# Every load of a decode-attention kernel in two halves of its columns, on two DMA queues

## Chip, cores, metric

One core of one Trainium2 chip. The metric is the device time of one execution in microseconds; lower is better.

## The reference

One token goes through four attention layers, which use two sets of caches and weights (A, B, A, B). Each layer reads all of its keys and values once, for a single query:

```python
# x: 1 x 1 x 640; 32 heads of 192; 8192 cached positions; all bf16
def _A_ref(x, k_cache, v_cache, wq, wo):                       # _B_ref is the same
    q = (x @ wq).reshape(B, Sq, Hq, Dh).transpose(0, 2, 1, 3)
    p = softmax(einsum("bhqd,bhkd->bhqk", q, k) * Dh ** -0.5)
    o = einsum("bhqk,bhkd->bhqd", p, v)
    return o.transpose(0, 2, 1, 3).reshape(B, Sq, Hq * Dh) @ wo
x = x + _A_ref(layernorm(x), ...)      # then B, then A again, then B again
```

## The kernel before

The kernel handles heads in pairs. Keys or values of a pair are 6.3 MB: 128 partitions with one contiguous row of 49,152 B each. They are loaded into a pool of eight slots of 24,576 B per partition; a slot is loaded again as soon as its reader is done.

Instructions are collected per engine, in program order. An operation first adds the waits for the events it needs to its engine's stream. `SP` is SyncE, `AC` ScalarE, `DV` VectorE (DVE), `PE` TensorE.

```python
class Queue:
    def op(self, fn, *events, sem=None, inc=1, signal=True, bank=()):
        ...
        self.wait(*events)                       # in front of fn, in this engine's stream
        ...
        self.counts[id(sem)] = self.counts.get(id(sem), 0) + inc
        self.items.append((fn, sem, inc))
        return sem, self.counts[id(sem)]         # the event: "sem has reached this count"
```

All loads but that of x are issued by SyncE, each as one transfer:

```python
def transfer(n):                                 # n: what to load, e.g. ("k", layer, pair, half)
    free = [freed[b] for b in before[n]]         # the readers of what lay in these slots
    ...
    if n[0] in "kv":
        h = 2 * pair(l, n[2])
        r = w[n[0]][0, h:h + 2].rearrange("h (p j) d -> (h p) (j d)", j=J)
        ...
        if whole(*n[:3]):                        # both slots in one transfer, 49,152 B a row
            f = lambda s: s.dma_start(pool[:, i * TS:(i + 2) * TS], r)
        else:                                    # one slot, 24,576 B a row
            f = lambda s: s.dma_start(t, r[:, n[3] * TS:(n[3] + 1) * TS])
    ...                                          # wq and wo in the same way
    return SP.op(f, *free, sem=semS[i], inc=16)

def ahead():                                     # after every step of the program:
    while issued[0] < len(plan):                 # load what is next in the plan,
        m = plan[issued[0]]
        if any(b not in freed for b in before[m]):
            return                               # as far as its slots' readers are in the program
        issued[0] += 1
        landed[m] = transfer(m)

ev_x = AC.op(lambda s: s.dma_start(x_bf[:], A_x[0, 0].rearrange("(p c) -> p c", c=DC)), sem=semX, inc=16)
ahead()
```

For each pair DVE multiplies the keys by the query, PE sums the products (reading the key slots), DVE and PE find the maximum, ScalarE takes the exponentials, PE multiplies by the values (reading the value slots), and DVE, PE and ScalarE gather the result in a row. ScalarE also copies the next pair's query (`q_sb`).

Of the kernel before, what the change touches and what calls it, by code (L numbers as in the profile page):

```python
# [63 lines left out]
PAIRS_W = 5  # L64
# [4 lines left out]
def build(nc, A_x, A_k, A_v, A_wq, A_wo, B_x, B_k, B_v, B_wq, B_wo, out):  # L69
    _, H, SK, DH = A_k.shape  # L70
    D = A_x.shape[-1]
    P = 128
    J = 2 * SK // P
    JU = J // 2
    DC = D // P
# [6 lines left out]
    PD = 2 * DH  # L82
    NW = PAIRS_W * PD // P
    QC = (NPAIR - 1) * PD
    QR = QC // 3
    TS = JU * DH
    QW = H * DH
    Q_PARTS = [(0, 2), (2, 2), (4, 1)]
    OI = PD // P
    NB = [0, 5, 0, 5]  # L90
# [4 lines left out]
                    wo=[NPAIR - PAIRS_W, 1, 1 + PAIRS_W], wol=0)  # L95
    ORDER = [FORWARD, FORWARD, FORWARD, BACKWARD]

    with ExitStack() as ctx:
        def sb(name, shape, dt):
            return ctx.enter_context(nc.sbuf_tensor(name, shape, dt))  # L100
# [4 lines left out]
        def sem(name):  # L105
            return ctx.enter_context(nc.semaphore(name))

        ident = sb("ident", [P, P], BF16)
        pool = sb("pool", [P, NSLOT * TS], BF16)
        slot = [pool[:, i * TS:(i + 1) * TS] for i in range(NSLOT)]  # L110
        wq0 = [sb(f"wq0{i}", [P, DC, PD], BF16) for i in range(2)]
        rows = sb("rows", [P, QR], BF16)
# [56 lines left out]
        AC = Queue(sem("pACT"))  # L169
        PO = Queue(sem("pPOOL"))  # L170
        SP = Queue()
        semS = [sem(f"semS{i}") for i in range(NSLOT)]
        semOL, semOB, semVQ, semX, semOUT = [sem(n) for n in ("semOL", "semOB", "semVQ", "semX", "semOUT")]

        e = PO.op(lambda g: g.memset(ident[:], 0.0))
# [6 lines left out]
        e = PO.op(lambda g: g.memset(mask, 0.0))  # L182
        for t in range(G):
            e = PO.op(lambda g, t=t: g.affine_select(
                out=mask, in_=mask, compare_op=ALU.not_equal, fill=1.0,
                base=-32 * t, pattern=[[-1, 2], [-2, VK]], channel_multiplier=1), e)
# [10 lines left out]
        def pair(l, p):  # L197
            return ORDER[l]["pairs"][p]
# [11 lines left out]
        def whole(kind, l, p):  # L210

            if kind == "t":
                return False
            if kind == "k":
                return l < 2 and p not in (PAIRS_W, 2 * PAIRS_W) or l == 3 and p > 1
            if p == NPAIR - 1:
                return False
            return l != 2 or p not in (0, PAIRS_W, 2 * PAIRS_W)
# [7 lines left out]
        for l in range(NL):  # L226
# [8 lines left out]
            for p in range(NPAIR):  # L235
# [17 lines left out]
                if p < NPAIR - 2:  # L253
                    if first_load("v", l, p) == (l, p):
                        plan += [("v", l, p, u) for u in range(2)]
                        if l == 2 and p == 1:
                            i = plan.index(("k", l, 1, 0))
# [33 lines left out]
        place, before, holder = {}, {}, [None] * NSLOT  # L291
# [29 lines left out]
        for i, n in list(enumerate(plan)):  # L321
            if n[0] == "v" and n[3] == 0:
                m = n[:3] + (1,)
# [8 lines left out]
        def wq_rows(l, g):  # L332

            c0, k = Q_PARTS[g]
            if l < 2:
                i = place[("wq", l, 0)] * TS
                return pool[:, i + c0 * QW:i + (c0 + k) * QW].rearrange("p (c n) -> p c n", c=k)
            return slot[place[("wq", l, g)]][:, 0:k * QC].rearrange("p (c n) -> p c n", c=k)

        def quarters(n):  # L340
            return n[0] == "v" and n[2:] == (NPAIR - 1, 1) and NB[n[1]] > 0

        def transfer(n):
            l = n[1]
            o = ORDER[l]
            w = W[l % 2]
            free = [freed[b] for b in before[n]]
            if n[0] == "wol":
                r0 = o["wol"] * PD
                return SP.op(lambda s: s.dma_start(  # L350
                    rows[:], w["wo"][r0:r0 + PD].rearrange("(p i) n -> p (i n)", p=P)),
                    *free, sem=semOL, inc=16)
            if n[0] == "t":
                return max(free, key=lambda e: e[1]) if free else None
            if n[0] == "wob":
                r0 = o["wo"][2] * PD
                return SP.op(lambda s: s.dma_start(
                    slot[place[("wo", l, 2)]][:, (NW - NB[l]) * D:NW * D],
                    w["wo"][r0:r0 + PAIRS_W * PD].rearrange("(p i) n -> p (i n)", p=P)[:, (NW - NB[l]) * D:]),
                    sem=semOB, inc=16)  # L360
            if n[0] == "vq":
                n = ("v", l, NPAIR - 1, 1)
            i = place[n]
            t = slot[i]
# [3 lines that stand above are left out]
                if quarters(n):  # L368
                    x = TS // 2
                    if n in landed:  # L370
                        return SP.op(lambda s: s.dma_start(t[:, x:], r[:, TS + x:]), sem=semVQ, inc=16)
                    return SP.op(lambda s: s.dma_start(t[:, 0:x], r[:, TS:TS + x]), *free, sem=semS[i], inc=16)
                if whole(*n[:3]):
                    if n[3] == 1:
                        return landed[n[:3] + (0,)]
                    f = lambda s: s.dma_start(pool[:, i * TS:(i + 2) * TS], r)
                else:
                    f = lambda s: s.dma_start(t, r[:, n[3] * TS:(n[3] + 1) * TS])
            elif n[0] == "wq" and l < 2:
                f = lambda s: s.dma_start(pool[:, i * TS:i * TS + DC * QW], w["wq"].rearrange("(p c) n -> p (c n)", c=DC))  # L380
            elif n[0] == "wq":
                c0, k = Q_PARTS[n[2]]
                f = lambda s: s.dma_start(
                    wq_rows(l, n[2]),
                    w["wq"][:, o["q1"] * PD:o["q1"] * PD + QC].rearrange("(p c) n -> p c n", c=DC)[:, c0:c0 + k, :])
            else:
                r0 = o["wo"][n[2]] * PD
                k = NW - NB[l] if n[2] == 2 else NW
                f = lambda s: s.dma_start(
                    t[:, 0:k * D], w["wo"][r0:r0 + PAIRS_W * PD].rearrange("(p i) n -> p (i n)", p=P)[:, 0:k * D])  # L390
            return SP.op(f, *free, sem=semS[i], inc=16)

        def need(n):

            while n not in landed:
# [3 lines that stand above are left out]
            return landed[n]  # L399

        def ahead():

            while issued[0] < len(plan):
                m = plan[issued[0]]
                if any(b not in freed for b in before[m]):
                    return
                issued[0] += 1
                landed[m] = transfer(m)
# [357 lines left out]
        for l in range(NL):  # L766
            ev_z, ev_true = layer(l, ev_z, ev_true)
        e = SP.op(lambda s: s.dma_start(out[0, 0].rearrange("(h n) -> h n", h=2), ev_z[0:33:32, :]), *ev_true, sem=semOUT, inc=16)
        SP.wait(e)
# [10 lines left out]
def bass_interleave_layers__gqa_block_cached__mha_block_cached__decode_kernel(  # L780
    nc: bass.Bass,
    A_x: bass.AP,
    A_k_cache: bass.AP,
    A_v_cache: bass.AP,
    A_wq: bass.AP,
    A_wo: bass.AP,
    B_x: bass.AP,
    B_k_cache: bass.AP,
    B_v_cache: bass.AP,
    B_wq: bass.AP,  # L790
    B_wo: bass.AP,
    out: bass.AP,
):
    build(nc, A_x, A_k_cache, A_v_cache, A_wq, A_wo, B_x, B_k_cache, B_v_cache, B_wq, B_wo, out)
# [28 lines left out]
```

## Time and profile before

| | before |
|---|---|
| median of 4 runs | 1983.51 us (1983.18 to 1985.16) |
| profiled span | 1980.6 us |
| loaded from HBM | 848.36 MB, 428 GB/s over the span |
| DMA packets | 26,786, nearly all on one queue (q1) |
| busy: PE, DVE, ACT | 65%, 61%, 7% |

The page gives busy shares of each engine, GB/s in 40 slices, and the packets that each DMA queue moved: a packet here is one partition's row of a transfer, or the 4 bytes that report a completion. Its lines stand in the prediction below.

### The profile page before, as it was taken

How to read it: one execution, taken by the hardware profiler on the slowest of the kernel's cores; microseconds unless marked ns; L12 is line 12 of the kernel's file. 1: busy time of each engine (PE TensorE's matmuls, PEld its weight loads, DVE VectorE, ACT ScalarE, POOL GpSimd, SP SyncE). 2: the span in 40 equal slices, each digit the busy share in tenths (PEclk: the TensorE clock that was granted, in tenths of full speed). 3: DMA queues.
4: the chain of work that ended last, by engine and by line, in shares of the span. 5: the costliest groups of instructions: out<-in, count | busy, mean ns of one | idle time of the engine just before them, and what ended most of it. 6: DMA issues, size and time to landing. Idle time of an engine off the chain costs nothing.

```text
span 1980.6 us, 13926 instructions
## 1 busy us (share of the span) xinstructions
PE 1282.8 (65%) x8335; PEld 148.6 (8%) x3249; DVE 1201.2 (61%) x1377; ACT 139.6 (7%) x462; POOL 4.5 (0%) x23
## 2 busy tenths in 40 slices
PE   3567476566466666666785675666676766667658
PEld 0001001000100100100020010010002001001001
DVE  3566466467166656566745565665764765665756
ACT  0000000000000000000010000000000100000000
POOL 0000000000000000000000000000000000000000
PEclk9787777778687777777887777877886877777778
DMA  9999999999999999999999999999999999999998
GB/s 413 437 432 430 430 430 432 436 430 428 435 431 431 430 435 433 428 433 433 427 408 432 427 430 431 430 430 431 431 431 428 436 429 434 432 432 431 431 434 364
DMA packets 26786, 849.25 MB, mean 429 GB/s; under 512 B 3042, under 2 KB 3044, under 8 KB 3812
## 3 DMA queue, kind: packets, MB, share of 16 engines
q1 hardware_dynamic: 26580, 848.38, 99.6%
q8 instruction: 45, 0.74, 0.2%
q14 instruction: 17, 0.14, 0.0%
q10 hardware_dynamic: 144, 0.00, 0.0%
HBM read 848.36 MB, written 0.00 MB: 428 GB/s over the span
## 4 chain that ended last, share of the span: by engine, by line
DMA 67%; PE 17%; DVE 15%; ACT 1%; issue 0%; SPq 0%
DMA pool<-in_B_k_cache_dram 27%; DMA pool<-in_A_v_cache_dram 22%; DMA pool<-in_A_k_cache_dram 13%; DVE pool L595 13%; PE S L58 7%; DMA pool<-in_B_v_cache_dram 6%; PE OY L58 5%; PE OY L674 3%; DVE acc L693 1%; ACT p_sb L632 1%; DVE s_sb L617 1%; PE OY L535 1%; PE S L608 0%; DVE m_bf L619 0%; PE QM L622 0%
## 5 line engine op out<-in xcount | busy, mean ns | idle before, releaser
L595 DVE TENSOR_TENSOR pool<-pool,q_sb 128x3072 bf16<-128x3072 bf16 x512 | 860.8, 1751 | 231.9 <-DMA pool<-in_B_k_cache_dram 133.3
L58 PE MATMUL S<-pool,ident 128*128 128x512 bf16 x2944 | 788.6, 425 | 20.4 <-DVE pool L595 18.8
L704 PE MATMUL TB<-acc,small 128*1 128x192 f32 x240 | 82.7, 495 | 212.0 <-DVE acc L693 212.0
L58 PE MATMUL OY<-pool,p_sb 128*16 128x512 bf16 x1920 | 198.8, 490 | 0.0
L608 PE MATMUL S<-pool,ident 128*128 128x512 bf16 x128 | 62.4, 488 | 207.7 <-DVE pool L595 207.6
L692 DVE TENSOR_SCALAR acc<-OY,small 128x192 f32<-128x192 f32 x64 | 26.7, 418 | 277.9 <-PE OY L58 248.0
L674 PE MATMUL OY<-pool,p_sb 128*16 128x512 bf16 (+1 forms) x1216 | 145.9, 488 | 64.3 <-DMA pool<-in_A_v_cache_dram 59.7
L693 DVE SCALAR_TENSOR_TENSOR acc<-OY,small,acc 128x192 f32<-128x192 f32 x424 | 177.0, 418 | 14.9
L617 DVE TENSOR_REDUCE s_sb<-S 128x64 f32<-128x512 f32 x128 | 87.8, 686 | 68.0 <-PE S L58 68.0
L524 ACT ACTIVATE q_sb<-QM 128x192 bf16<-128x192 f32 x60 | 19.8, 330 | 952.4 <-PE QM L518 952.4
L715 ACT ACTIVATE rows<-TB,small 1x192 bf16<-1x192 f32 x120 | 43.1, 405 | 587.7 <-PE TB L704 587.7
L688 DVE RECIPROCAL small<-TB 1x2 f32<-1x2 f32 x64 | 11.2, 175 | 94.7 <-PE TB L647 75.3
L632 ACT ACTIVATE p_sb<-s_sb,small 64x128 bf16<-64x128 f32 x128 | 55.7, 435 | 160.9 <-DVE small L626 160.1
L608 PEld LDWEIGHTS S<-pool,ident 128*128 128x128 bf16 x128 | 12.9, 101 | 682.9 <-DVE pool L595 619.9
L647 PE MATMUL TB<-small,ones 128*1 128x2 f32 x120 | 11.4, 165 | 74.1 <-ACT p_sb L632 74.1
L674 PEld LDWEIGHTS OY<-pool,p_sb 128*16 128x16 bf16 (+1 forms) x1216 | 38.9, 105 | 207.4 <-issue 133.1
L622 PE MATMUL QM<-ident,m_bf 128*64 128x64 bf16 x128 | 14.1, 217 | 54.4 <-DVE m_bf L619 53.8
L704 PEld LDWEIGHTS TB<-acc,small 128*1 128x1 f32 x240 | 19.8, 102 | 311.2 <-DVE acc L693 284.0
L535 PE MATMUL OY<-oT,pool 128*128 128x1 bf16 x825 | 34.9, 178 | 2.5 <-ACT oT L580 2.5
L626 DVE TENSOR_REDUCE small<-QM 128x1 f32<-128x64 f32 x64 | 14.3, 224 | 35.2 <-PE QM L622 35.2
L535 PEld LDWEIGHTS OY<-oT,pool 128*128 128x128 bf16 x825 | 33.9, 131 | 4.5 <-ACT oT L580 3.2
L518 PEld LDWEIGHTS QM<-rows,one_b 1*64 1x64 bf16 x120 | 6.2, 100 | 347.1 <-issue 341.2
(75 smaller groups left out, 205.0 us busy)
## 6 DMA issues: line engine op xcount, KB each, us to landing
pool<-in_B_k_cache_dram SPq DMA_DIRECT2D x28, 6144.0 KB, 38.1
pool<-in_B_v_cache_dram SPq DMA_DIRECT2D x28, 6144.0 KB, 33.5
pool<-in_A_v_cache_dram SPq DMA_DIRECT2D x27, 6144.0 KB, 27.6
pool<-in_A_k_cache_dram SPq DMA_DIRECT2D x34, 3072.0 KB, 19.9
pool<-in_A_k_cache_dram SPq DMA_DIRECT2D x14, 6144.0 KB, 36.5
pool<-in_A_v_cache_dram SPq DMA_DIRECT2D x10, 3072.0 KB, 14.3
pool<-in_B_k_cache_dram SPq DMA_DIRECT2D x8, 3072.0 KB, 22.4
pool<-in_A_wo_dram SPq DMA_DIRECT2D x6, 2400.0 KB, 22.1
```

Of the source, the lines that this page charges most:

```text
L58: return t.add_instruction(mybir.InstMatmult(name=t.bass.get_next_instruction_name(), engine=mybir.EngineType.PE, ins=[t.lower_ap(rhs), t. ...
L524: lambda a: a.activation(q_sb[i][:], QM[:, 0:DH], ACT.Copy), e, last["q"][i], bank=QMu)
L535: e = PE.op(lambda t, i=i, c=c, f=y_first[0], fin=n[0] == "wol" and i == k - 1: t.matmul(YB[:, c:c + 1], lhsT=t3[:, i, c:D:DC], rhs=o[:, i ...
L595: e = DV.op(lambda v, d0=d0: v.tensor_tensor(k3[:, :, d0:d0 + QD], kin[:, :, d0:d0 + QD], q_sb[qi][:, d0:d0 + QD].unsqueeze(1).broadcast_t ...
L608: t.matmul(S[:, :], lhsT=ident[:], rhs=k3[:, :, d0:d0 + R], start=True, stop=fin) if d0 == 0 else
L617: lambda v, u=u: v.tensor_reduce(s[:, u * JU:(u + 1) * JU], SP_[u][:].rearrange("p (j r) -> p j r", r=R), AX.X, ALU.add), ev_S[p, u], last ...
L632: ev_p[p] = AC.op(lambda a, h=h, r=r: a.activation(p_sb[par][r, :, h], s[r, :], ACT.Exp, bias=negm[par][r, 0:1], accum_out=l_col[par][r, h ...
L674: t.matmul(o, lhsT=x, rhs=y, start=f, stop=fin) if c == 0 else
L692: v.tensor_scalar(acc[:], O[:, 0:DH], pick[:, 0:1], None, ALU.mult) if i == 0 else
L693: v.scalar_tensor_tensor(out=acc[:], in0=O[:, i * DH:(i + 1) * DH], scalar=pick[:, i:i + 1], in1=acc[:], op0=ALU.mult, op1=ALU.add)), e if ...
L704: e = PE.op(lambda t, h=h: t.matmul(TB[96:97, C_O + h * DH:C_O + (h + 1) * DH], lhsT=half[:, h:h + 1], rhs=acc[:], start=True, stop=True), ...
L715: last["TO"] = last["row_written"] = AC.op(lambda a, h=h: a.activation(orow[:, o0 + h * DH:o0 + (h + 1) * DH], TB[96:97, C_O + h * DH:C_O ...
```

## The change

Every load becomes two, each of half the columns over all 128 partitions; one half is issued by SyncE, the other by ScalarE, on the same semaphore. The intent is to have two queues feed the DMA engines and two engines issue. The two queues now add to the same semaphores, so they share one table of counts.

```diff
         SP = Queue()
+        SP.counts = AC.counts
...
             free = [freed[b] for b in before[n]]
+
+            def move(dst, src, sem):
+
+                if len(dst.shape) == 3 and dst.shape[1] == 2:
+                    parts = [(slice(None), i) for i in range(2)]
+                else:
+                    m = dst.shape[-1] // 2
+                    parts = [(slice(None),) * (len(dst.shape) - 1) + (c,) for c in (slice(0, m), slice(m, 2 * m))]
+                for q, x in zip((SP, AC), parts):
+                    e = q.op(lambda s, x=x: s.dma_start(dst[x], src[x]), *free, sem=sem, inc=16)
+                return e
...
                 if whole(*n[:3]):
                     if n[3] == 1:
                         return landed[n[:3] + (0,)]
-                    f = lambda s: s.dma_start(pool[:, i * TS:(i + 2) * TS], r)
+                    f = pool[:, i * TS:(i + 2) * TS], r
                 else:
-                    f = lambda s: s.dma_start(t, r[:, n[3] * TS:(n[3] + 1) * TS])
+                    f = t, r[:, n[3] * TS:(n[3] + 1) * TS]
...            (wq, wo and the last values in the same way)
-            return SP.op(f, *free, sem=semS[i], inc=16)
+            return move(*f, semS[i])
```

More of the change, by code (lines that the diff above doesn't have):

```diff
@@ L347, in transfer @@
             free = [freed[b] for b in before[n]]
+            def move(dst, src, sem):
[7 more added lines that the diff above has]
+                return e
             if n[0] == "wol":
                 r0 = o["wol"] * PD
-                return SP.op(lambda s: s.dma_start(
-                    rows[:], w["wo"][r0:r0 + PD].rearrange("(p i) n -> p (i n)", p=P)),
-                    *free, sem=semOL, inc=16)
+                return move(rows, w["wo"][r0:r0 + PD].rearrange("(p i) n -> p (i n)", p=P), semOL)
             if n[0] == "t":
@@ L356, in transfer @@
                 r0 = o["wo"][2] * PD
-                return SP.op(lambda s: s.dma_start(
-                    slot[place[("wo", l, 2)]][:, (NW - NB[l]) * D:NW * D],
-                    w["wo"][r0:r0 + PAIRS_W * PD].rearrange("(p i) n -> p (i n)", p=P)[:, (NW - NB[l]) * D:]),
-                    sem=semOB, inc=16)
+                return move(slot[place[("wo", l, 2)]][:, (NW - NB[l]) * D:NW * D],
+                            w["wo"][r0:r0 + PAIRS_W * PD].rearrange("(p i) n -> p (i n)", p=P)[:, (NW - NB[l]) * D:], semOB)
             if n[0] == "vq":
@@ L370, in transfer @@
                     if n in landed:
-                        return SP.op(lambda s: s.dma_start(t[:, x:], r[:, TS + x:]), sem=semVQ, inc=16)
-                    return SP.op(lambda s: s.dma_start(t[:, 0:x], r[:, TS:TS + x]), *free, sem=semS[i], inc=16)
+                        free = []
+                        return move(t[:, x:], r[:, TS + x:], semVQ)
+                    return move(t[:, 0:x], r[:, TS:TS + x], semS[i])
                 if whole(*n[:3]):
@@ L375, in transfer @@
                         return landed[n[:3] + (0,)]
-                    f = lambda s: s.dma_start(pool[:, i * TS:(i + 2) * TS], r)
+                    f = pool[:, i * TS:(i + 2) * TS], r
                 else:
-                    f = lambda s: s.dma_start(t, r[:, n[3] * TS:(n[3] + 1) * TS])
+                    f = t, r[:, n[3] * TS:(n[3] + 1) * TS]
             elif n[0] == "wq" and l < 2:
-                f = lambda s: s.dma_start(pool[:, i * TS:i * TS + DC * QW], w["wq"].rearrange("(p c) n -> p (c n)", c=DC))
+                f = pool[:, i * TS:i * TS + DC * QW], w["wq"].rearrange("(p c) n -> p (c n)", c=DC)
             elif n[0] == "wq":
                 c0, k = Q_PARTS[n[2]]
-                f = lambda s: s.dma_start(
-                    wq_rows(l, n[2]),
-                    w["wq"][:, o["q1"] * PD:o["q1"] * PD + QC].rearrange("(p c) n -> p c n", c=DC)[:, c0:c0 + k, :])
+                f = (wq_rows(l, n[2]),
+                     w["wq"][:, o["q1"] * PD:o["q1"] * PD + QC].rearrange("(p c) n -> p c n", c=DC)[:, c0:c0 + k, :])
             else:
@@ L388, in transfer @@
                 k = NW - NB[l] if n[2] == 2 else NW
-                f = lambda s: s.dma_start(
-                    t[:, 0:k * D], w["wo"][r0:r0 + PAIRS_W * PD].rearrange("(p i) n -> p (i n)", p=P)[:, 0:k * D])
-            return SP.op(f, *free, sem=semS[i], inc=16)
+                f = t[:, 0:k * D], w["wo"][r0:r0 + PAIRS_W * PD].rearrange("(p i) n -> p (i n)", p=P)[:, 0:k * D]
+            return move(*f, semS[i])
         def need(n):
```

## The prediction

> **What bounds the kernel now.** I read the page first: bytes and GB/s, busy shares, then the chain that ended last.
>
> ```profile
> PE 1282.8 (65%) x8335; PEld 148.6 (8%) x3249; DVE 1201.2 (61%) x1377; ACT 139.6 (7%) x462; POOL 4.5 (0%) x23
> GB/s 413 437 432 430 430 430 432 436 430 428 435 431 431 430 435 433 428 433 433 427 408 432 427 430 431 430 430 431 431 431 428 436 429 434 432 432 431 431 434 364
> DMA packets 26786, 849.25 MB, mean 429 GB/s; under 512 B 3042, under 2 KB 3044, under 8 KB 3812
> q1 hardware_dynamic: 26580, 848.38, 99.6%
> DMA 67%; PE 17%; DVE 15%; ACT 1%; issue 0%; SPq 0%
> ```
>
> No compute engine is above 65%, while one queue (q1, SyncE's) keeps the 16 DMA engines busy for 99.6% of the span, at 427 to 437 GB/s in all slices but the first, the 21st and the last. The chain still gives 33% to PE, DVE and ACT. Is that time in which the DMA engines stand still? The windows view, in stretches of 20 us, answers (columns: stretch, length, busy time and count of PE, PEld, DVE, ACT, POOL, granted clock, DMA share, GB/s):
>
> ```profile
> 0.00:20.00 20.00, 0.00 (x0) 0.00 (x0) 2.01 (x3) 0.00 (x0) 2.30 (x19) 1.00 0.96 393
> 40.00:60.00 20.00, 14.58 (x99) 0.81 (x23) 14.75 (x19) 1.31 (x5) 0.00 (x0) 0.93 1.00 431
> 60.00:80.00 20.00, 12.93 (x46) 0.54 (x6) 14.04 (x10) 0.72 (x2) 0.00 (x0) 0.67 1.00 433
> ...
> 1000.00:1020.00 20.00, 17.17 (x216) 9.01 (x204) 4.04 (x15) 1.59 (x5) 0.55 (x1) 0.66 0.95 382
> ...
> 1960.00:1980.00 20.00, 14.51 (x175) 5.28 (x139) 5.09 (x14) 2.42 (x9) 0.00 (x0) 0.95 0.68 284
> ```
>
> It is not: the DMA share is 1.00 in the middle whatever the compute does, and 0.95 even at the worst seam between layers. I counted the packet records of the trace to be sure: fewer than 16 packets are in flight for about 2.5 us before the first byte, about 1 us in the middle (around 1000 us) and 5.7 us after the last load. So the chain's PE and DVE pieces run beside transfers already queued, and the kernel is a stream of 848.36 MB with some 9 us around it. Only what changes the packets' own duration, or empties the queue, can move the end.
>
> **What the Trainium skill says.** All four places are in its page "DMA: Bandwidth & Descriptors". (1) Section "Issuing engines are not separate DMA queues": transfers started by different engines share the same 16 DMA engines and interleave, so a second issuer saves sequencer time only. Here that time is 0.33 to 0.44 us per issue on a SyncE that has nothing else to do. (2) "Where 436 GB/s comes from" sets a ceiling of 435.2 GB/s for the 16 ports. The trace agrees: undisturbed stretches show 433. (3) "Queues, rings and completion order": each DMA engine takes turns between queues packet by packet. The trace shows it in the load of x, the only load that ScalarE issues now, at the same moment as SyncE's first:
>
> ```profile
> 0.73 0.41 ACTq L417 DMA_DIRECT2D x_bf<-in_A_x_dram  x1
> 0.73 0.39 SPq L380 DMA_DIRECT2D pool<-in_A_wq_dram  x1
> 22.36 0.17 DVE L419 CAST small<-x_bf 128x5 f32<-128x5 bf16 x1 [16.85 <-DMA x_bf<-in_A_x_dram]
> ```
>
> These 1.2 KB take 21.6 us, because each of an engine's eight packets of x waits behind one packet of wq: 61,440 B, 2.27 us in the packet records (8 x 2.27 = 18.1 us, plus the start and a slow first packet). A turn here (one packet of wq and one of x) is 2.27 us too, against 2.264 to 2.268 between two packets of wq alone: a change of queue costs nothing that can be seen. (4) "Why small descriptors are slow (HBM only)" gives a fixed overhead of about 3 cycles per packet. The records agree that there is one and give its size: from start to start on one DMA engine, packets of 49,152, 24,576 and 12,288 B take about 1812, 908.5 and 457 ns. A line through these is 0.03676 ns per byte (435 GB/s over 16 engines) plus about 5 ns per packet. The 4-byte packet that signals completion takes 6 ns.
>
> **The change part by part.** The bytes stay the same. The program's counts per transfer double.
> - *Data packets.* The page lists 182 SyncE transfers, 181 of them loads. Each is 128 partition rows in one packet each, except four wq pieces of two rows, which are split between these rows and get no new packet. So 177 x 128 = 22,656 packets more. At 5 ns, over 16 engines: 22,656 x 5.2 / 16 / 1000 = 7.4 us. All of it lies on the bounding stream.
> - *Completion packets.* 181 transfers x 16 = 2,896 more, at 6 ns over 16 engines: 1.1 us.
> - *Issue.* SyncE's 182 issues stay; ScalarE gets 181 at some 0.35 us (estimate from SyncE's) = 63 us on an engine 7% busy. Beside other work: 0.
> - *Waits on ScalarE.* Its stream is in order, so each wait for a free buffer now stands between its activations. Read in program order per pair: copy of the next q, wait for the last key product, issue, the two exponentials, wait for the last value product, issue, the two row copies. Each activation depends on something that comes after the event just waited for: the exponentials need the maximum over these products, and the row copies need the gather after the value product. So no activation is held up, and ScalarE's halves are issued at most 1 us behind SyncE's: 0.
> - *Start.* Packets of wq are now 30,720 B, so x's eight turns last 8 x 1.14 us and x lands near 13 us. But ScalarE's half of wq stands behind x, and then takes turns with SyncE's half of the first keys: 8 x (1.14 + 0.91) = 16.4 us more, so wq is whole near 29 us (21.4 now). The first query matmul (25.5 us now) comes some 3.6 us later, and so does the next load, issued at 31.4 us. The first two loads keep the engines busy until about 36.3 us, and an issue needs 1.8 us to its first byte: 31.4 + 3.6 + 1.8 = 36.8. A gap of about 0.5 us.
> - *Tail.* After the last value quarter lands (1973.9 us) there are 6.7 us of compute and the store. The halves arrive together, so 0, give or take 1 us.
>
> Sum: 7.4 + 1.1 + 0.5 = 9 us, on 1983.8: 1992.8. I take 1991, since turns between two queues may hide a little of the 5 ns.
>
> A cross-check by the windows view: in 1040 to 1480 us (third layer), where keys already move in 3,072 KB transfers, the mean of the 22 stretches is 430.5 GB/s; in 540 to 1000 us (second layer, mostly whole transfers) it is 431.7. That is 0.28% for halving about half of the bytes; for all of them 0.55% or 11 us. It points the same way and to the same size.
>
> **Rivals.**
> - *Two queues fill holes.* For it: the chain has 33% outside DMA, and transfers wait for buffers (SyncE's longest kinds of wait: 731 us and 410 us in total). Against it: with a busy share of 1.00 there are no holes. The very best is 848.36 MB at 435.2 GB/s = 1949 us, plus the 9 us around it: 1958, which is 1.3% faster. A more likely gain is a few us: 1978 to 1984.
> - *ScalarE becomes the bottleneck or starves its queue.* For it: 63 us of issues and some 120 waits in an engine on the path from scores to values.
>
> ```profile
> ACT p_sb L632 <- DVE small L626: 160.1, 64, 23.6
> ...
> DVE pool L595 <- DMA pool<-in_B_k_cache_dram: 133.3, 31, 13.4
> DVE pool L595 <- DMA pool<-in_A_k_cache_dram: 97.2, 27, 9.8
> ```
>
>   Against it: the order above, and slack. DVE waits up to 13.4 us for keys, about 4 us a time, so the exponentials could be some us late before a buffer is freed late. And the backlog covers it: a 6,144 KB load takes about 14.5 us by itself, but lands 28 to 38 us after issue. If I misread one dependence, it is some us in each of 64 pairs: 2000 to 2100 us.
> - *Large packets of two queues disturb each other.* The load of x shows only 10-byte packets in turn. Against my calm speaks the instruction queue (q8, 45 packets of 16 KB): such a packet takes 1.07 us where its size asks for 0.6, and a load packet after it is about 0.46 us longer. If every turn between two load queues cost that, it would be thousands of us; I hold it for a property of those fetches, since they come singly and not from a full queue. Even 15 ns per turn would be 45,000 x 15 / 16 = 42 us: 2035.
>
> **Range and chances.** Most weight is on the packet cost fully paid (about 1993), partly hidden (1985 to 1990), or paid with a few us of gaps (to 2000). Range 1982 to 2001. Faster by 2% (below 1944) lies under the floor of 1949: 0.01. Slower by 2% (above 2023) needs one of the last two rivals: 0.06. Within 2%: 0.93.
>
> **What would show it.** Two queues of some 424 MB each, about 52,000 packets together, over 5,800 under 512 B; undisturbed stretches near 431 to 432 GB/s with the DMA share at 1.00; x landing near 13 us and the first matmul on wq near 29; ScalarE's waits for PE and DVE nearly the same in sum; the transfers' time to landing unchanged within some us. I am wrong if the DMA share falls under 1.00 in the middle (starved queue), if a 24,576 B packet takes turns longer than about 910 ns, or if GB/s rises above 434.

## The result, and the profile after

| | before | after |
|---|---|---|
| median | 1983.51 us (4 runs) | 1996.87 us (4 runs, 1996.18 to 1998.04) |
| profiled span | 1980.6 us | 1994.4 us |
| ratio | | 1.0066, 95% interval 1.0049 to 1.0084 |

A ratio is the mean time of one kernel's runs over that of the other's in the same rounds, so it is not quite the ratio of the medians quoted. Executions over 1.5% slower than the fastest of the same kernel are left out of the means. The outcome lies in the range; it is 0.7% slower, 13.4 us, where the sum forecast 9 and the figure finally taken, 1991, some 7.5.

The page after: GB/s in 40 slices, the packets, and the queues (q1 is SyncE's, q10 ScalarE's).

```profile
GB/s 401 432 430 429 430 429 429 430 431 427 430 431 430 428 430 430 429 430 431 426 405 430 426 422 426 429 425 423 430 427 424 431 428 432 429 431 429 430 430 365
DMA packets 52340, 849.28 MB, mean 426 GB/s; under 512 B 5938, under 2 KB 6964, under 8 KB 9524
q1 hardware_dynamic: 26068, 424.19, 50.0%
q10 hardware_dynamic: 26208, 424.19, 49.9%
```

The bytes are the same; the packets have gone from 26,786 to 52,340. 34 of the 38 middle slices are lower, mostly by 1 to 5 GB/s: the loss is spread over the whole run. The windows after (same columns as in the prediction) show that the DMA engines are as busy as before:

```profile
0.00:20.00 20.00, 1.15 (x4) 1.00 (x4) 3.92 (x18) 1.28 (x1) 2.87 (x20) 1.00 0.92 380
20.00:40.00 20.00, 7.91 (x77) 1.27 (x26) 4.81 (x4) 2.28 (x2) 0.00 (x0) 0.98 0.98 413
40.00:60.00 20.00, 14.08 (x97) 0.80 (x23) 14.72 (x19) 1.31 (x5) 0.00 (x0) 0.93 1.00 431
60.00:80.00 20.00, 11.87 (x43) 0.54 (x6) 12.85 (x9) 0.72 (x2) 0.00 (x0) 0.67 1.00 430
```

In the third and fourth row the share is 1.00 and the rate 431 and 430: busy all the time, moving as much or a little less than before (431 and 433). (The view counts a packet whole where it starts, so a share can be some hundredths off, and over 1.) Of the stretches after the first, only that from 20 to 40 us is below 1.00; it was 1.00 before, at 433 GB/s. ScalarE's waits after (engine, line, what it waited for: total us, times, longest) answer to the row of `p_sb` quoted in the prediction:

```profile
ACT p_sb L640 <- DVE small L634: 160.7, 64, 23.7
```

160.7 us against 160.1: the exponentials are not held up by the 181 issues in ScalarE's stream.

### The profile page after: what moved, and what is told of

Its sections match the earlier page's. It is cut to its first block, busy times and chain, and to the rows that moved or that the text cites. A ratio compares the mean times of both kernels' runs of the same rounds, so it can differ in the third digit from the quotient of the medians.

```text
span 1994.4 us, 14113 instructions
## 1 busy us (share of the span) xinstructions
PE 1285.7 (64%) x8335; PEld 149.1 (7%) x3249; DVE 1201.9 (60%) x1377; ACT 139.8 (7%) x462; POOL 4.5 (0%) x23
## 4 chain that ended last, share of the span: by engine, by line
DMA 68%; PE 16%; DVE 15%; ACT 1%; issue 0%; ACTq 0%
DMA pool<-in_B_k_cache_dram 27%; DMA pool<-in_A_v_cache_dram 22%; DMA pool<-in_A_k_cache_dram 13%; DVE pool L603 13%; PE S L58 6%; DMA pool<-in_B_v_cache_dram 5%; PE OY L58 5%; PE OY L682 3%; DVE acc L701 1%; DMA pool<-in_A_wq_dram 1%; ACT p_sb L640 1%; DVE s_sb L625 1%; PE S L616 0%; PE OY L543 0%; DVE m_bf L627 0%
## 5 line engine op out<-in xcount | busy, mean ns | idle before, releaser
L640 ACT ACTIVATE p_sb<-s_sb,small 64x128 bf16<-64x128 f32 x128 | 55.7, 435 | 161.5 <-DVE small L634 160.7
```

What stands on the lines that cost most here:

```text
L640: ev_p[p] = AC.op(lambda a, h=h, r=r: a.activation(p_sb[par][r, :, h], s[r, :], ACT.Exp, bias=negm[par][r, 0:1], accum_out=l_col[par][r, h ...
```

## The experiments

The theory after the two traces, called P in the expectations: every packet costs a fixed time on its DMA engine, whatever its size and its queue. I added up the durations of the load packets in the records of both traces, took off what overlapped, and divided by 16 engines: +13.3 us after the change, of which 1.1 us are completions and 12.2 us the 22,656 data packets, 8.6 ns each. The rivals are T (turns between two queues cost) and S (ScalarE, or the start).

**e1: the halves on one queue.**

```diff
-                for q, x in zip((SP, AC), parts):
+                for q, x in zip((SP, SP), parts):
```

> The same halves of columns, but both on SyncE's queue: the packets of the change without its second queue. Theory P (every packet costs the same fixed time, about 8.6 ns, worked out from the two traces as 12.2 us of 16 engines over 22,656 packets, whatever queue it is on): +13 us, 1997, a ratio of 1.0065. Theory T (a packet costs the 5 ns of the prediction, the rest is the turn between two queues): +8.5 us, 1992, ratio 1.0043. Theory S (it is ScalarE's waits and issues that cost, or x and wq at the start): 1984 to 1988.

Measured: 1995.73 us, 5 runs, before 1983.11 in the same rounds, ratio 1.0060 (1.0048 to 1.0073). Its packets:

```profile
DMA packets 52339, 849.27 MB, mean 426 GB/s; under 512 B 5938, under 2 KB 6964, under 8 KB 9524
```

With ScalarE's queue out of it, 12.6 us of the loss are still there. Two queues are not its main cause; as many packets as in the change are. Rival S is out: it had expected 1984 to 1988.

**e3: every transfer whole, all on ScalarE.**

```diff
-                parts = <the two halves of the change>
-                for q, x in zip((SP, AC), parts):
+                parts = [(slice(None),)]
+                for q, x in zip((AC,), parts):
```

> No split, every transfer whole on ScalarE's queue, SyncE issues only the store. Theories P and T: 1983 to 1985, no packet more and no turns; x is first in the same queue and lands within 4 us instead of 21.6, wq at 21 to 22 us as before, which the stream does not notice. Theory S (waits and issues in ScalarE's ordered stream hold up its activations): twice the transfers per issue of the change's ScalarE, but as many waits, so +4 us or more, 1988 or above.

Measured: 1983.80 us, ratio 1.0003 (0.9991 to 1.0016). All of the loads' issues and waits in ScalarE's ordered stream cost nothing here, as the prediction had argued from the order of that stream. x landed early (its first reader ran at 5.4 us instead of 22.4) and the first query matmul ran at 22.6 us instead of 25.5, and that did not change the time either: the stream of loads sets the end.

**e5: a dose, quarters on SyncE alone.**

```diff
-                    m = dst.shape[-1] // 2
-                    parts = <two slices of m columns>
-                for q, x in zip((SP, AC), parts):
+                    m = dst.shape[-1] // 4
+                    parts = <four slices of m columns>
+                for q, x in zip((SP,) * 4, parts):
```

(The two-row pieces of wq are cut into two halves of each row.)

> A dose: quarters of the columns, all four on SyncE's queue, 68,992 data packets and 8,688 completion packets more than before. Theory P at 8.6 ns and 6 ns over 16 engines: 37.1 + 3.3 = +40 us, 2024, ratio 1.020. Theory T at 5.2 ns: 22.4 + 3.3 = +26 us, 2009, ratio 1.013. DMA share 1.00 in the middle either way; SyncE's issues 724 x 0.35 = 250 us, still hidden.

Measured: 2020.65 us, ratio 1.0188 (1.0174 to 1.0202). Its page's packets, and a stretch of its windows to set against the rows above:

```profile
DMA packets 104470, 849.32 MB, mean 420 GB/s; under 512 B 11730, under 2 KB 14804, under 8 KB 53716
```
```profile
40.00:60.00 20.00, 16.38 (x100) 0.98 (x23) 13.27 (x14) 1.31 (x5) 0.00 (x0) 0.86 1.01 425
```

Still a full DMA share, and 425 GB/s where the halves had 431. The page's packets have risen by 77,684, and the time by 37.5 us: 37.5 x 16 / 77,684 = 7.7 ns per packet. For e1 the same working gives 12.6 x 16 / 25,553 = 7.9 ns. The cost is proportional to the number of packets over a threefold dose, at a little under the expectation (40 us over the same packets is 8.3 ns, completions included). One number of the expectation was missed: SyncE's issues took 692 us in all, not 250. 152 of them lasted over 1 us, up to 9.6 us, against 0.33 us before. Nothing else waits on SyncE, and the DMA share stayed full, so it cost nothing here.

**e2: two queues with whole transfers.** Values on ScalarE's queue, except those of each layer's last pair; everything else on SyncE's.

```diff
+                parts = [(slice(None),)]
-                for q, x in zip((SP, AC), parts):
+                for q, x in zip((AC if n[0] == "v" and n[2] < NPAIR - 1 else SP,), parts):
```

> No split: every transfer whole as before, but the values of all pairs except the last of each layer are issued by ScalarE, so that both queues carry large packets (about 45% of the bytes on ScalarE's). Theory P: no packet more, so 1983 to 1985. Theory T (some 3 ns per turn, at most 23,700 packets over 16 engines): +2 to +4.5 us, 1986 to 1988. If two queues spoil the order in which transfers land, keys late by up to a value load of 14 us, DVE's waits for keys rise from 13 us to over 20 and the DMA share falls under 1.00.

Measured: 2028.16 us, ratio 1.0231 (1.0214 to 1.0247), far above what P and T expected, and with not one packet more than before. Its windows at the worst places:

```profile
500.00:520.00 20.00, 13.78 (x218) 7.21 (x180) 5.71 (x15) 1.89 (x7) 0.00 (x0) 0.70 0.81 336
980.00:1000.00 20.00, 14.19 (x58) 0.51 (x7) 16.72 (x14) 1.31 (x5) 0.00 (x0) 0.91 0.82 351
1220.00:1240.00 20.00, 7.51 (x41) 0.63 (x13) 8.68 (x12) 0.72 (x2) 0.00 (x0) 0.62 0.72 296
2000.00:2020.00 20.00, 17.04 (x208) 5.48 (x151) 6.55 (x17) 2.15 (x8) 0.00 (x0) 1.00 0.28 107
```

Here the DMA share does fall, to 0.72 to 0.82: the DMA engines ran out of packets, mostly around the seams between layers, in the third layer, and at the end. That is the third outcome in the expectation. DVE's longest wait for B's keys rose to 18.9 us, from 13.4, though not over 20. In one queue a load that is needed sooner is served first; in two, it shares the engines with one that is needed later. That this sharing is the cause fits the waits but was not tested by itself. Turns between large packets do not cost: in the packet records a packet of 49,152 B takes 1814 ns from start to start when it is followed by one of the other queue, and 1815 ns in the kernel before. So this speaks against T, even though the run's time missed the numbers of both theories.

**e0: the change again, as the control.** No edit.

> The change itself again, as the control beside the three other runs of this call. 1996 to 1998, a ratio of 1.0066 as at first. The one-queue halves gave 1.0060; if the ratio stays 1.0063 to 1.0070, two queues cost some 1 us more than one, and if it falls to 1.0060, nothing.

Measured: 1997.18 us, ratio 1.0070 (1.0057 to 1.0083). The change lies some 1 to 2 us above the one-queue halves both times, but the intervals overlap.

**e4: quarters on two queues.** As e5, with `(SP, AC, SP, AC)`.

> The dose on two queues: quarters of the columns, two on each queue, as many packets as the quarters on SyncE alone (2020.65 us, ratio 1.0188). Theory P (fixed cost per packet, queue without effect): the same within 2 us, 2019 to 2023. Theory T (each turn between queues costs about 1 ns more): 100,000 turns over 16 engines, +6 us, 2027.

Measured: 2030.28 us, ratio 1.0236 (1.0223 to 1.0249), above T's number even, and outside P's. But the packet records show the load packets taking the same time in both (2006.5 us of 16 engines, overlap taken off); what has grown is the time in which engines stand idle, from 6.9 to 12.6 us within the stream, and that lies at the end. The timeline of ScalarE there (start, length, what; in brackets the idle time before it):

```profile
1972.01 11.71 ACTq L360 DMA_DIRECT2D pool<-in_B_v_cache_dram  x4
1983.75 6.59 ACTq L360 DMA_DIRECT2D pool<-in_B_wo_dram  x2
1990.39 0.33 ACT L534 ACTIVATE q_sb<-QM 128x192 bf16<-128x192 f32 x1 [28.82 <-issue]
```

And the chain that ended last, in order of time (start, length, what):

```profile
1972.88 4.38 ACTq L360
...
1977.30 6.42 ACTq L360
...
1983.75 6.11 ACTq L360
...
1990.39 0.34 ACT q_sb L534
```

Single issues on ScalarE take 4.4, 6.4 and 6.1 us instead of 0.35: ScalarE is held in its own DMA issues, and the copy of the last pair's query stands behind them. In e5 that copy ran at 1978.7 us; here it is 12 us later, and DVE, which multiplies the last keys by it, with it. This is the rival of the prediction that ScalarE becomes the bottleneck; the change itself is spared it (its longest issue takes 1.0 us), the quarters are not. This is not peculiar to ScalarE or to a second queue: SyncE's issues are held in the same stretch here (up to 6.4 us), were held near the end of e1 (5 over 1.5 us, up to 6.3) and in e5. These runs put 363 or more transfers on one queue, where the change puts 182 on each. That the number of transfers queued is the cause was not tested; e7, with as many at half the rate, was not held (1.2 us at most). In e1 and e5 the held engine had nothing else to do.

**e10: the same, but the last layer's quarters all on SyncE.** As e4, with `((SP,) * 4 if l == 3 else (SP, AC, SP, AC))`.

> The quarters on two queues (2030.28 us), but in the last layer all four on SyncE. If its 10 us over the quarters on SyncE alone (2020.65) came from ScalarE being held in its own issues near the end (one q copy 12 us late in the trace): 2020 to 2023. If they came from turns between queues over the whole run: three quarters of them stay, 2027 to 2029.

Measured: 2021.77 us, ratio 1.0188 (1.0174 to 1.0202), that of e5 to the last digit. The 10 us come from the last layer, where the trace of e4 shows ScalarE held. Turns between queues in the other three layers cost nothing that can be measured (the interval is 3 us to either side), and T is out.

**e6 and e7: rows instead of columns.** To keep two transfers but no new data packets, the cut goes between partitions.

```diff
-                parts = <the two halves of the change>
+                parts = [(slice(64 * i, 64 * i + 64),) for i in range(2)]
-                for q, x in zip((SP, AC), parts):         # e6
+                for q, x in zip((SP, SP), parts):         # e7
```

> Two halves and two queues, but the cut is between partitions 64 rows each: packets stay whole rows of up to 49,152 B and as many as before, only the 2,896 completion packets are added. Theory P: +1.1 us, 1984 to 1986, so the loss is gone although both queues and all issues of the change stay. If the cost lay in two queues, two issues or two completions: 1990 or above. A danger to the reading: 64 rows may load the DMA engines or the memory's ports otherwise; then GB/s in undisturbed stretches is off 433.

> The same cut between partitions, both halves on SyncE's queue, one after the other. Theory P: +1.1 us, 1984 to 1986. If a transfer of 64 rows writes only half of the memory's ports at a time, the second half cannot run beside the first in one queue and GB/s falls well under 433 (to half at worst, 3900 us).

Measured: e6 3650.60 us (3587.20 to 3664.23), ratio 1.8215; e7 3983.17 us (3886.80 to 4025.77). Their spread is over 1.5%, so e7 has no ratio; against a doubling that does not matter. The packets of e6 and of e7:

```profile
DMA packets 29684, 849.28 MB, mean 232 GB/s; under 512 B 5938, under 2 KB 5940, under 8 KB 6708
DMA packets 29683, 849.27 MB, mean 211 GB/s; under 512 B 5938, under 2 KB 5940, under 8 KB 6708
```

As a control the pair failed, in the way that both expectations had named as a danger: 211 GB/s (232 in e6) is about half of the 429 of before, with the DMA engines busy throughout. A transfer to 64 neighbouring partitions runs at about half the rate, and a second queue that fills the other 64 at the same time wins back only a tenth.

**e11: even and odd partitions.** The control again, with halves that both reach over all 128 partitions; on two queues.

```diff
-                parts = <the two halves of the change>
+                parts = [(slice(i, 128, 2),) for i in range(2)]
```

> The control that the cut at partition 64 failed to be: even partitions on SyncE's queue and odd on ScalarE's, so packets stay whole rows, as many as before, on two queues with both issues and completions. If 64 neighbouring rows were slow because they lie on half of the memory's ports, rows spread over all 128 go at 433 GB/s, and theory P gives +1.1 us plus the start's gap: 1984 to 1987. If any transfer of 64 rows is slow: 3500 us again, and the control stays open.

Measured: 1986.65 us, ratio 1.0010 (0.9996 to 1.0024), and the full rate:

```profile
DMA packets 29684, 849.28 MB, mean 428 GB/s; under 512 B 5938, under 2 KB 5940, under 8 KB 6708
```

This is the cleanest test of P. Both queues, both issues and both completions of the change are there; only the rows are whole, and 11 of its 13.4 us are gone. The start differs too: x's first reader runs at 5.4 us, the next load is issued at 31.3 us, and the gap of the change at 35 us (0.5 to 1.5 us, see below) is not there. So some 10 of the 11 us are the data packets'. e11 shows too that what e6 and e7 suffered from is which 64 rows a transfer names, not their number. Whether it is the partitions or the rows in HBM was not separated: they change together.

**e8: the start as before.** The change, with the first wq and the first keys whole on SyncE.

```diff
+                first = n in (('wq', 0, 0), ('k', 0, 0, 0), ('k', 0, 0, 1))
...
+                parts = [(slice(None),)] if first else parts
-                for q, x in zip((SP, AC), parts):
+                for q, x in zip(((SP, SP) if first else (SP, AC)), parts):
```

> The change, but layer 0's wq and first keys whole on SyncE's queue as before, so that ScalarE's half of wq no longer stands behind x. Theory (the change is 12 us of packets plus a gap of 0.5 to 1.6 us near 36 us after the start, where the next load comes after the first two have landed): 1995.5 to 1996.5, ratio 1.0060 to 1.0064, with no gap in the 20 to 40 us stretch (DMA share 1.00, where the change has 0.93 and 0.98) and the first matmul on wq back at 25 to 26 us from 29.3. Rival (the last microsecond over the one-queue halves is the two queues themselves): ratio stays 1.0068 to 1.0070.

Measured: 1996.46 us, ratio 1.0063 (1.0051 to 1.0076): inside the theory's numbers, but the interval holds the rival's too. The first matmul on wq is back at 25.3 us as expected; the DMA share from 20 to 40 us is 0.97 and not the expected 1.00, though the packet records show hardly an engine without a packet there. Inconclusive.

## Why the prediction was right, point by point

- **What bounds the kernel.** Right. The end moved with the packets' total duration (e1, e5, e11), and not with what was done to the issue (e3).
- **Data packets.** The mechanism was right and the count exact: the page's packets rose by 25,554, forecast were 22,656 + 2,896 = 25,552. The size was too small. "about 5 ns per packet" came from starts to starts of 1812, 908.5 and 457 ns, which are low values of the records before; their medians are 1815, 911 and 459, and a line through those has some 7 ns per packet. The doses measure 7.7 to 7.9 per packet, completions included. At 8.1 ns for data packets ((12.6 - 1.1) x 16 / 22,656 from e1) the term is 11.5 us and not 7.4: this term was mis-sized, by nearly all of the 4 us that the sum fell short. The cross-check by windows, 11 us, came nearer than the sum.
- **Completion packets.** 1.1 us was forecast. Their duration is unchanged in the records (6 ns from start to start), and e11, which has them and no new data packets, is 0.1% slower, 2 us (the interval reaches from -1 to 5).
- **Issue and waits on ScalarE: 0.** Right for the change (e3; 160.7 us of waits against 160.1). It is not a rule: in e4 issues of 0.35 us became 4 to 6 us and held ScalarE for 18 us. What was overlooked is that an issue can be held. (The sum of 181 issues at 0.35 us came out: 67 us in the trace after.)
- **Start.** Right for x and wq, in the trace after; the size of the gap is partly luck:

```profile
0.74 0.41 ACTq L425 DMA_DIRECT2D x_bf<-in_A_x_dram  x1
...
1.18 0.45 ACTq L358 DMA_DIRECT2D pool<-in_A_wq_dram  x1
...
12.75 0.17 DVE L427 CAST small<-x_bf 128x5 f32<-128x5 bf16 x1 [7.23 <-DMA x_bf<-in_A_x_dram]
...
29.33 1.01 PE L484 MATMUL QM<-pool,xb 128*64 128x192 bf16 x10 [13.99 <-DMA pool<-in_A_wq_dram]
```

  x lands 12.0 us after issue (forecast: near 13 us) and the first matmul on wq runs at 29.3 us (forecast: near 29). The next load is issued at 34.8 us (forecast: 35.0). The gap of about 0.5 us is there too, but by two errors that offset each other. The first byte came 1.0 us after the issue, not 1.8: in the records a load issued at 34.78 us has its first packet at 35.75, and in the trace before the load issued at 0.73 us has it at 1.75. And the engines began to run dry at 35.4 us, not 36.3. In windows of 2 us, before and after:

```profile
34.00:36.00 2.00, 0.00 (x0) 0.00 (x0) 0.00 (x0) 0.09 (x1) 0.00 (x0) 0.94 1.02 442
36.00:38.00 2.00, 0.00 (x0) 0.00 (x0) 1.28 (x1) 0.00 (x0) 0.00 (x0) 0.50 0.96 418
```
```profile
34.00:36.00 2.00, 1.49 (x24) 0.09 (x3) 0.00 (x0) 0.41 (x1) 0.00 (x0) 1.00 0.80 295
36.00:38.00 2.00, 0.00 (x0) 0.00 (x0) 1.66 (x1) 1.45 (x1) 0.00 (x0) 1.00 0.85 307
```

  The share falls to 0.80 and 0.85, 0.4 + 0.3 = 0.7 us lost. In the repeated run, e0, it fell to 0.63, 0.78 and 0.85, 1.5 us.
- **Tail.** Right within the microsecond allowed: from the landing of the last value quarter to the end of the span 6.7 us before (1973.9 to 1980.6), the same after (1987.7 to 1994.4).
- **"turns between two queues may hide a little of the 5 ns".** Wrong. They hide nothing (e1 against the change, e5 against e10). They add nothing that can be seen either: the prediction's sign of being wrong, a 24,576 B packet that takes longer than about 910 ns, reads 912 ns after (median, next packet of the other queue), but 911 before.
- **Two queues fill holes.** Refuted as argued: no slice after is above 432 GB/s, and there were no holes to fill.

In sum: 11.5 us of data packets, 1.1 us of completions and 0.5 to 1.5 us at the start make 13 to 14 us, against 13.4 measured. What stays open is the last microsecond between e1 and the change, which these intervals, about 3 us to either side, can't assign, and how e2's DMA engines came to be without packets.

## What to carry to other kernels

Look first whether the DMA engines have a hole: where their share was 1.00 and the rate flat, as here, a second queue had nothing to add, and the number of packets (partition rows times pieces of a row) is what is left to count. A row cut in two costs one more packet per partition, and a second queue brought two losses: e2 lost 45 us, probably because loads no longer came in the order of need (not tested by itself), and in e4 ScalarE, which also issued loads, was held in the issue (+10 us). Where a transfer must be cut, give each piece whole rows spread over all partitions (e11, 428 GB/s); cut at partition 64 it ran at 211 to 232.

## What the Trainium skill lacked or had wrong

- "DMA: Bandwidth & Descriptors", section "Why small descriptors are slow (HBM only)": it gives a fixed cost of about 3 cycles per packet, works it out for 256 B, and finds joining descriptors worthwhile only up to 256 B. Here a row cut in two or four costs 7.7 to 7.9 ns for each added packet (completions included), with most rows of 6,144 to 24,576 B, and that is 12.6 us of 1983 in e1: fewer and larger rows still pay at these sizes.
- The same page, section "Issuing engines are not separate DMA queues", speaks only of the sequencer time that a second issuer saves. What it can lose is not said there: issues of 4.4 to 6.4 us held ScalarE's own work (e4, +10 us), and with values and keys on two queues the DMA share fell to 0.72 in places (e2, +45 us; why was not tested).
